# An output product split after nine of its fifteen steps, and rules by slot for a hand-written order: a gated mix of two memory-attention branches on one core

## The chip, the core and the metric

The kernel runs on one core of a Trainium2 chip. Its engines are TensorE (PE in the profile; PEld is its loading of weights), VectorE (DVE), ScalarE (ACT), GpSimd (POOL) and SyncE (SP, which issues every DMA here). The metric is device time of one execution in microseconds.

## What is computed

Two branches, A and B, each do the following with weights of their own. Their results are mixed token by token.

```python
# x: 2048 tokens x 640; 32 heads of 20; 4 segments of 512 tokens
q, k, v = x @ wq, x @ wk, x @ wv
M, z = 0, 0
for s in range(4):
    logits = einsum("hqd,hkd->hqk", qs, ks) * 20 ** -0.5 + causal_mask
    a_dot = softmax(logits) @ vs
    a_mem = (phi(qs) @ M) / (phi(qs) @ z + 1e-6)      # phi(t) = t + 1 if t > 0 else exp(t)
    o = sigmoid(beta) * a_mem + (1 - sigmoid(beta)) * a_dot
    M, z = M + phi(ks).T @ vs, z + phi(ks).sum(tokens)
branch = o @ wo
# after both branches
g = sigmoid((x * gate_w).sum(-1))
out = g * branch_A + (1 - g) * branch_B
```

## The kernel before

**Tiling.** A window t is one branch of one segment: t = 0 to 7, with branch t % 2 and segment t // 2. In a window the 32 heads are taken four at a time; such a group is a quad, i = 0 to 63, eight to a window. The 640 features are five blocks of 128 (k or m = 0 to 4). A product of 640 by 640 with 512 tokens is done block by block: for each output block m it has 15 steps, five blocks k by three terms, because each operand is split into a high and a low part (high x high, low x high, high x low). The products are q, k, v and o of every window.

**Halves.** Most matmuls use only 64 of the 128 rows of the array, so that two streams, one for each half, run at once. `product` (L577) gives a unit whose steps exist once for each half: one half does its steps first, the other follows into the same PSUM bank after a lag, `UP_LAG` (0.3). A step of both halves is costed at `STEP` = 0.2335. `whole` (L160) emits a matmul over all 128 rows.

**One quad.** S units (L962, five to a quad) make scores for the row maximum, which DVE reads (L980). The maxima go through a small transpose and a DMA into two extra rows of `qst` (L1013 to L1033). T units (L1052, five to a quad) make the transposed scores less the maximum; ACT takes the exponential (L1075) and POOL masks it (L1076). They need a place for the result: ten tiles of their own (`own_p`), or rows borrowed from the pool `big` of 27 rows, where `p_room` (L1039) allows that. When all ten masked tiles are there, `pv_unit` (L1091) does the weighted sum with v on the whole array (L1103, 32 matmuls). `fin_unit` (L1146) transposes it back, DVE weights it, and POOL adds it to the memory part in `O`. When the heads of a feature block k are complete, `o_transpose` (L1187) gives the pair `OTs[t, k]`, ready when its low part is subtracted (L1196). The output product of a window reads these five pairs.

**Order.** The program is written by a planner inside the kernel: it runs a clock with costs for each operation, and emits each instruction when its model says that the inputs are there. What is emitted is a fixed order for each engine; nothing is decided on the chip. Products ("jobs", L322 to L327) are filler, taken in order by `fill_gen` (L1224); `marks[i]` says how much filler is done before slot i begins. In slot i the main loop (L1361 on) places the ten units of `ORDER`: T units of quad i, S units of quad i + 2, each after `fill_to` a target, spread over `SPAN` = 1.010 of the slot; the weighted sum of quad i - 1 falls due at its start. Units with low priority (memory reads, updates, transposes for them) are held back while DVE has more than `CALM` = 2.38 us queued (`start_late`, L1244). T units may borrow rows when at least `BORROW` + 2 = 10 are free and nobody waits for rows. These settings are the same in all 66 slots.

**The last output product** (t = 7) has no window behind it to be filler for, so `job_last` (L880) does its five blocks m side by side in five banks, with whole matmuls, k by k as the pairs come:

```python
    yield from hold_on(lambda: (t, KT - 2) in OTs, "last")
    ...
    for k in range(KT):
        yield from hold_on(lambda: (t, k) in OTs, "last")
        ...
        for m in range(KT):
            ...
            for j, (w, o) in enumerate(((wh, oh), (wl, oh), (wh, ol))):
```

The result of branch A for the same segment, already in `part`, is loaded (L890) and added (L901), and the sum is stored (L903).

Of the kernel before, what the change touches and what calls it, by code (L numbers as in the profile page):

```python
# [12 lines left out]
F32 = mybir.dt.float32  # L13
# [29 lines left out]
def tile_gated_mix_infini_attn(  # L43
# [43 lines left out]
    idle = []  # L87
    DONE = {"A": 0.14, "D": 0.11, "G": 0.1, "S": 0.0}
# [69 lines left out]
    UP_LAG = 0.3  # L158
# [147 lines left out]
    BORROW = 8  # L306
# [20 lines left out]
    jobs += [(7, "last", m) for m in range(KT)]  # L327
# [3 lines left out]
    def cost(kind):  # L331
        return 60 * STEPV if kind == "v" else 15 * STEP
# [28 lines left out]
    def stage(i):  # L361
# [3 lines left out]
        t, kind, m = jobs[i]  # L365
        src = weights[t % 2][kind if kind in "qkv" else "o"]
# [29 lines left out]
        def got(w):  # L396
            w3 = w.rearrange("p (k n) -> p k n", n=P)

            def landed():
                if kind == "last" and m == KT - 1:  # L400
                    wvhl.want(1, lambda pair: split_hi(tuple(x[:, :, :P] for x in pair)))
                else:
                    whl.want(1, split_hi, prio=i)
# [475 lines left out]

    def job_last(t):  # L880

        s = t // 2
        yield from hold_on(lambda: (t, KT - 2) in OTs, "last")
        parts, pps = {}, {}
        for m in range(KT):
            def got_pt(tile, m=m):
                if (s, m) not in part_there:
                    at(clk[0] + 0.5, lambda: got_pt(tile, m))
                    return
                dma(0.7, lambda: nc.sync.dma_start(  # L890
                    out=r32(tile), in_=part[s][P * m:P * (m + 1), :]), lambda: parts.__setitem__(m, tile))

            big.want((F32,), got_pt, prio=3)

        def finish(m):
            def got(ot):
                def take():
                    if m not in parts:
                        at(clk[0] + 0.3, take)
                        return  # L900
                    put("D", 0.63, lambda: nc.vector.tensor_tensor(  # L901
                        out=r32(ot), in0=pps[m], in1=r32(parts[m]), op=ALU.add), lambda: dma(
                            0.7, lambda: nc.sync.dma_start(  # L903
                                out=outT[P * m:P * (m + 1), L * s:L * (s + 1)], in_=r32(ot)), prio=2), prio=2)

                take()

            big.want((F32,), got, prio=2)

        for k in range(KT):  # L910
            yield from hold_on(lambda: (t, k) in OTs, "last")
            oh, ol = OTs[t, k]
            for m in range(KT):
                i = job_index[t, "last", m]
                yield from hold_on(lambda: i in split, "split")
                wh, wl = split[i]
# [3 lines left out]
                for j, (w, o) in enumerate(((wh, oh), (wl, oh), (wh, ol))):  # L920
                    yield from hold_on(lambda: not any((*firsts, *seconds, *lane_ops)), "last")
                    whole(STEP, lambda: nc.tensor.matmul(  # L922
                        pps[m], lhsT=w[:, k, :], rhs=o, start=(k == 0 and j == 0), stop=(k == KT - 1 and j == 2)))
# [115 lines left out]
    def p_room():  # L1039
        return len(own_p) > 1 or len(big.free) >= BORROW + 2 and not big.queue  # L1040

# [169 lines left out]
    def begin(i):  # L1211
# [3 lines left out]
        if kind == "last" and m == 0:  # L1215
            for j in range(i, len(jobs)):
                stage(j)
# [6 lines left out]
    def fill_gen():  # L1224
        for i, (t, kind, m) in enumerate(jobs):
# [7 lines left out]
            if i < len(HEAD0):  # L1233
# [4 lines left out]
                        "last": lambda: job_last(t) if m == 0 else ()}[kind]()  # L1238
# [5 lines left out]
    def start_late(keep):  # L1244
        for x in late:
            prio, _, cost, ok, fn = x
            if len(bank.free) <= (0 if prio <= 0 else keep) or (prio > 2 and load["D"] > CALM):
                continue
# [4 lines left out]
    def start_unit(half):  # L1253

        u = start_late(KEEP)
# [11 lines left out]
    def lane_step(half):  # L1267
# [24 lines left out]
        if u:  # L1292
# [3 lines left out]
            if not u["ops"][half]:  # L1296
                firsts[half] = None
                u["at"] = lane[half] + UP_LAG
# [45 lines left out]
    CALM, KEEP, UNIT = 2.38, 0, 1  # L1344
    ORDER = "TSTSTSTSTS"
    SPAN = 1.010
# [14 lines left out]
    for i in range(66):  # L1361
        fill_to(marks[i])
        if i == 0:
            for j in range(LEAD):
                for n in range(5):
                    when_ready(UNIT, S(j, n), "S")
# [3 lines left out]
        todo = list(ORDER if i else "TSTSTSTSTS")  # L1370
        at_ = {"S": 0, "T": 0}
        for j in range(len(ORDER)):
            fill_to(marks[i] + SPAN * (j + 1) / len(ORDER) * (marks[i + 1] - marks[i]))
# [66 lines left out]
```

## Time and profile before

| | |
|---|---|
| median of three runs | 1073.05 us (1070.78 to 1073.85) |
| the profiled execution | 1072.62 us, span 1070.8 us |
| granted TensorE clock, mean | 0.998 |
| busy: PE, PEld, DVE, ACT, POOL | 1054.6, 885.3, 763.2, 658.1, 584.3 us |
| HBM read, written | 131.43 MB, 73.40 MB |

The span is the time from the first to the last instruction of the program, and the profiled execution's own time has what lies around it as well. Busy times are unions of an engine's instructions. Ends of matmuls are modelled, so a busy PE may still be fed thinly.

### The profile page before, as it was taken

To read this page: it belongs to the slowest core of one execution; us is meant where nothing else is said; L and a number is where in the kernel's file an instruction comes from. 1 tells how busy PE (TensorE), PEld (TensorE's weight loads), DVE (VectorE), ACT (ScalarE), POOL (GpSimd) and SP (SyncE) were. 2 spreads that over 40 slices of the span, in tenths; PEclk is the share of its full clock that TensorE was granted. 3 is DMA by queue.
4 is the path that set the end of the run, shared out by engine and by line. 5 is a ranking of instruction groups with operands and counts; after the bars stand their busy time and mean duration, and the time that the engine had idled before them with its cause. 6 is when DMAs were issued, how large, how long until landed. Compare 5 with 4: busy or idle time off the path is not lost.

```text
span 1070.8 us, 31710 instructions
## 1 busy us (share of the span) xinstructions
PE 1054.6 (98%) x11689; PEld 885.3 (83%) x11689; DVE 763.2 (71%) x2724; ACT 658.1 (61%) x1330; POOL 584.3 (55%) x1045
## 2 busy tenths in 40 slices
PE   7999999999999999999999999999999999999998
PEld 6877888988989889888798888888878887889855
DVE  3597776659767698665887768856777867877751
ACT  5276656668665576655765557655665657576670
POOL 4273636467364574566645557555764537555470
PEclk9999999999999999999999999999999999999999
DMA  6985587477565786664847468657575765857521
GB/s 235 308 282 146 192 242 216 129 236 241 157 202 146 197 273 189 195 196 141 253 144 220 150 180 275 179 180 228 146 229 164 238 179 170 253 167 194 166 83 49
DMA packets 110026, 207.95 MB, mean 194 GB/s; under 512 B 12464, under 2 KB 16560, under 8 KB 109872
## 3 DMA queue, kind: packets, MB, share of 16 engines
q1 hardware_dynamic: 109872, 205.93, 63.8%
q8 instruction: 92, 1.51, 0.6%
q14 instruction: 62, 0.51, 0.2%
HBM read 131.43 MB, written 73.40 MB: 191 GB/s over the span
## 4 chain that ended last, share of the span: by engine, by line
PE 93%; DMA 2%; ACT 2%; DVE 1%; POOL 1%; issue 1%; SPq 0%; ACTq 0%; POOLq 0%; DVEq 0%
PE bank L580 52%; PE bank L1103 13%; PE bank L993 7%; PE bank L1083 7%; PE bank L724 4%; PE bank L764 3%; PE bank L686 3%; PE bank L922 2%; PE bank L625 1%; DMA row<-in_xT_dram 1%; ACT p L1075 1%; DVE bank L980 1%; DMA kst<-kd 1%; PE bank L1018 1%; DMA wst<-in_a_wk_dram 0%
## 5 line engine op out<-in xcount | busy, mean ns | idle before, releaser
L980 DVE CUSTOM_DVE_ANT_0 bank<-bank,tri 128x384 f32<-128x384 f32 (+3 forms) x1024 | 475.7, 519 | 160.6 <-PE bank L993 134.1
L580 PE MATMUL bank<-row,wh 64*128 64x512 f32 x2220 | 509.6, 406 | 1.2 <-ACT p L1075 0.5
L1075 ACT ACTIVATE p<-bank 128x512 f32<-128x512 f32 x602 | 330.8, 599 | 171.4 <-PE bank L1083 136.5
L1076 POOL TENSOR_SCALAR_AFFINE_SELECT p<-p 128x256 f32<-128x256 f32 (+1 forms) x602 | 219.1, 372 | 279.1 <-ACT p L1075 268.1
L580 PEld LDWEIGHTS bank<-row,wh 64*128 64x128 f32 x2220 | 312.0, 186 | 17.9 <-issue 3.4
L580 PE MATMUL bank<-row,wl 64*128 64x512 f32 x1110 | 292.9, 400 | 0.0
L409 POOL TENSOR_TENSOR wl<-wst,wh 128x640 fp32r<-128x640 f32 x115 | 180.0, 1570 | 49.8 <-ACT wh L407 49.4
L580 PE MATMUL bank<-wvh,row 64*128 64x320 f32 x1280 | 201.7, 316 | 0.3 <-ACT p L1075 0.3
L993 PE MATMUL bank<-kst,qst 60*128 60x384 f32 (+3 forms) x1024 | 183.2, 321 | 0.1
L1083 PE MATMUL bank<-qst,kst 62*128 62x384 f32 (+3 forms) x1024 | 179.5, 320 | 0.2
L580 PEld LDWEIGHTS bank<-row,wl 64*128 64x128 f32 x1110 | 166.6, 185 | 7.0 <-issue 1.2
L580 PEld LDWEIGHTS bank<-wvh,row 64*128 64x128 f32 x1280 | 161.5, 185 | 3.5 <-issue 1.6
L1103 PE MATMUL bank<-p,vst 128*32 128x128 f32 (+3 forms) x1964 | 151.2, 434 | 0.0
L980 DVE DVE_READ_ACCUMULATOR2_ANT mx<- 128x1 f32 x1024 | 145.1, 142 | 0.0
L993 PEld LDWEIGHTS bank<-kst,qst 60*128 60x128 f32 x1024 | 127.9, 185 | 10.3 <-issue 1.6
L1083 PEld LDWEIGHTS bank<-qst,kst 62*128 62x128 f32 x1024 | 127.9, 185 | 9.0 <-issue 1.6
L1103 PEld LDWEIGHTS bank<-p,vst 128*32 128x32 f32 x1964 | 59.7, 110 | 88.1 <-issue 64.0
L580 PE MATMUL bank<-wvl,row 64*128 64x320 f32 x640 | 113.5, 312 | 0.0
L407 ACT CAST wh<-wst 128x640 fp32r<-128x640 f32 x119 | 85.5, 738 | 23.7 <-PE bank L580 11.9
L580 PEld LDWEIGHTS bank<-wvl,row 64*128 64x128 f32 x640 | 88.2, 185 | 0.8 <-issue 0.6
L549 DVE TENSOR_TENSOR row<-bank,row 128x512 fp32r<-128x512 f32 x80 | 54.8, 688 | 36.8 <-ACT row L537 17.7
L724 PE MATMUL bank<-ident,row 64*128 64x64 f32 x752 | 79.6, 226 | 1.2 <-DVE mx L980 0.8
(91 smaller groups left out, 1252.5 us busy)
## 6 DMA issues: line engine op xcount, KB each, us to landing
qd<-row SPq DMA_DIRECT2D x120, 256.0 KB
kd<-row SPq DMA_DIRECT2D x120, 256.0 KB
qst<-qd SPq DMA_DIRECT2D x128, 240.0 KB
kst<-kd SPq DMA_DIRECT2D x128, 240.0 KB
wst<-in_a_wq_dram SPq DMA_DIRECT2D x20, 320.0 KB
wst<-in_a_wk_dram SPq DMA_DIRECT2D x20, 320.0 KB
wst<-in_b_wq_dram SPq DMA_DIRECT2D x20, 320.0 KB
wst<-in_b_wk_dram SPq DMA_DIRECT2D x20, 320.0 KB
```

The source lines that it names most:

```text
L407: put("A", 0.66, lambda: nc.scalar.copy(wh, w3), lambda: put(lo_eng, lo_cost, lambda: lo.tensor_tensor(out=wl, in0=w3, in1=r32(wh), op=ALU ...
L409: lambda: lo.tensor_tensor(out=wl, in0=w3, in1=r32(wh), op=ALU.subtract), end, prio=3), prio=6)
L549: put("D", 0.63, lambda: nc.vector.tensor_tensor(out=lo, in0=src, in1=r32(hi), op=ALU.subtract), out, prio=1)
L580: return nc.tensor.matmul(bank_of, lhsT=w[ROWS[half]], rhs=x_[ROWS[half]], start=start, stop=stop)
L686: return nc.tensor.matmul(pm[:, a - h0:c - h0, :].rearrange("p h e -> p (h e)"), lhsT=r32(pqTs[t, m][ROWS[half], P * n:P * (n + 1)]), rhs= ...
L724: return nc.tensor.transpose(px[:, n, r], block(n)[r], ident[r, r])
L980: put("D", w / 960.0 + 0.112, lambda: nc.vector.tensor_tensor_reduce(out=sc[:, off:off + w], in0=sc[:, off:off + w], in1=tri[:, L - w:], s ...
L993: lane_ops[half].append((w * 0.000458, lambda pair=pair, qb=qb, off=off, w=w, r=r, sc=sc: nc.tensor.matmul(sc[:, off:off + w], lhsT=q[r, p ...
L1075: put("A", 0.49, lambda: nc.scalar.activation(pt, sc, AF.Exp, scale=SCALE), lambda: (bank.give(sc), put("G", 0.05 + 0.16 * len(todo), lamb ...
L1076: "G", 0.05 + 0.16 * len(todo), lambda: nc.gpsimd.affine_select(out=blocks, in_=blocks, pattern=[[0, len(todo)], [1, P]], base=0, channel_ ...
L1083: lane_ops[half].append((w * 0.000458, lambda pair=pair, kb=kb, off=off, w=w, r=r, sc=sc: nc.tensor.matmul(sc[:, off:off + w], lhsT=k[r, p ...
L1103: nc.tensor.matmul(po[32 * j:32 * j + 32, P * kb:], lhsT=vst[t % 2][:, kb, h * E1:h * E1 + 32], rhs=pts[i, n, f][0][:, off:off + w], start ...
```

## The change

The jobs of the last product become five "early" ones, one for each m, and one "last". An early job is an ordinary product of nine steps: k = 0, 1, 2 (`SOON` = 3), both halves of the array, due as soon as the first three pairs exist. Its sum is added to the row of `part` on DVE, kept in that row (`kept`), and its bank is given back. The job "last" then does the other six steps of each m side by side as before, and adds its banks to the kept rows in place. The special staging of all weights at the start of the last product goes: the weights come by the look-ahead of four jobs, as for others.

The constants `ORDER`, `SPAN`, `CALM`, `UP_LAG` and `BORROW` become fields of a table, `RULES`, by slot, in the order: order of units, span, calm, lag, room. A rule holds until a later slot has one. `KEEP` and `UNIT` are replaced by their values.

```diff
@@ -85,6 +85,46 @@
     load = {e: 0.0 for e in "ADGS"}
     dma_free = [0.0, 0.0]
     idle = []
+
+
+    RULES = {
+        0: "TSTSTSTSTS 1.010 2.38 0.30 4",
+        2: "SSTSTSTSTT 1.010 2.38 0.41 4",
+        3: "TSTSTSTSTS 0.932 2.38 0.30 8",
+        5: "TSTSTSTSTS 0.947 2.38 0.30 8",
+        6: "TSTSTSTSTS 1.010 1.90 0.26 8",
+        7: "TTSSTTSSTS 1.010 1.62 0.40 8",
+        9: "TSTSTSTSTS 1.010 2.38 0.30 8",
+        15: "TSTSTSTSTS 0.994 2.09 0.32 4",
+        16: "TSTSTSTSTS 1.029 2.38 0.37 8",
+        17: "TSTSTSTSTS 1.010 2.38 0.31 8",
+        18: "TSTSTSTSTS 0.936 3.13 0.30 8",
+        23: "TTSTSTSTSS 0.931 2.38 0.41 4",
+        24: "TSTSTSTSTS 1.010 2.38 0.30 8",
+        26: "TSTSTSTSTS 0.941 2.69 0.31 8",
+        28: "TSTSTSTSTS 0.947 3.15 0.30 8",
+        30: "TSTSTSTSTS 1.010 2.38 0.30 8",
+        31: "STSTSTSTST 0.948 3.28 0.30 6",
+        32: "TSTSTSTSTS 0.997 2.38 0.30 8",
+        33: "TSTSTSTSTS 1.010 3.21 0.30 8",
+        35: "TSTSTSTSTS 1.010 2.38 0.30 8",
+        39: "SSTSTSTSTT 1.010 2.38 0.30 4",
+        41: "TSTSTSTSTS 1.010 2.38 0.30 8",
+        44: "TSTSTSTSTS 0.971 2.38 0.30 8",
+        48: "TSTSTSTSTS 1.010 2.38 0.30 8",
+        49: "TSSTTSSTTS 1.010 2.38 0.38 8",
+        50: "TSTSTSTSTS 1.010 2.38 0.30 8",
+        51: "TSTSTSTSTS 1.010 2.38 0.38 8",
+        54: "TSTSTSTSTS 1.010 2.38 0.30 8",
+        56: "TSSTTSSTTS 1.010 2.38 0.30 8",
+        59: "TSTSTSTSTS 1.010 3.16 0.33 8",
+        60: "SSSTSTSTTT 0.922 1.82 0.30 8",
+        61: "TTSSTTSSTS 1.010 3.55 0.27 8",
+        62: "TSTSTSTSTS 1.010 2.38 0.30 8",
+        63: "SSTSTSTSTT 1.010 2.38 0.30 8",
+        65: "SSTSTSTSTT 0.950 2.38 0.36 8",
+    }
+    rule = {}
     DONE = {"A": 0.14, "D": 0.11, "G": 0.1, "S": 0.0}
 
     def at(time, fn):
@@ -155,7 +195,6 @@
     lane_ops = [deque(), deque()]
     firsts = [None, None]
     seconds = [deque(), deque()]
-    UP_LAG = 0.3
 
     def whole(dur, emit):
         now[0] = max(now[0], lane[0], lane[1]) + dur
@@ -303,7 +342,6 @@
     wvhl = Store([tuple(sb.tile([P, KT, VN], F32R, tag=f"wv{c}", name=f"wv{c}", bufs=1) for c in "hl")])
 
     own_p, pts = list(range(10)), {}
-    BORROW = 8
 
 
     HEAD0 = [("q", 0), ("k", 0), ("q", 1), ("k", 1)]
@@ -324,12 +362,14 @@
     jobs = [(0, kind, m) for kind, m in HEAD0]
     for t in range(8):
         jobs += window_jobs(t)
-    jobs += [(7, "last", m) for m in range(KT)]
+    jobs += [(7, "early", m) for m in range(KT)]
+    jobs += [(7, "last", 0)]
+    SOON = 3
     job_index = {j: i for i, j in enumerate(jobs)}
 
 
     def cost(kind):
-        return 60 * STEPV if kind == "v" else 15 * STEP
+        return 60 * STEPV if kind == "v" else 3 * SOON * STEP if kind == "early" else 15 * STEP
 
     def window_cost(t):
         return sum(cost(kind) for _, kind, _ in window_jobs(t))
@@ -363,6 +403,8 @@
             return
         staged.add(i)
         t, kind, m = jobs[i]
+        if kind == "last":
+            return
         src = weights[t % 2][kind if kind in "qkv" else "o"]
         lo_eng, lo = ("D", nc.vector) if i < 4 else ("G", nc.gpsimd)
         lo_cost = 0.9 if i < 4 else 1.6
@@ -397,7 +439,7 @@
             w3 = w.rearrange("p (k n) -> p k n", n=P)
 
             def landed():
-                if kind == "last" and m == KT - 1:
+                if kind == "early" and m == KT - 1:
                     wvhl.want(1, lambda pair: split_hi(tuple(x[:, :, :P] for x in pair)))
                 else:
                     whl.want(1, split_hi, prio=i)
@@ -877,50 +919,65 @@
 
         yield from product(pp, terms, STEP, done)
 
+    kept = {}
+
+    def job_early(t, m):
+
+        i = job_index[t, "early", m]
+        s = t // 2
+        pt = []
+
+        def got_pt(tile):
+            if (s, m) not in part_there:
+                at(clk[0] + 0.5, lambda: got_pt(tile))
+                return
+            dma(0.7, lambda: nc.sync.dma_start(
+                out=r32(tile), in_=part[s][P * m:P * (m + 1), :]), lambda: pt.append(tile), prio=need[i] + 4)
+
+        big.want((F32,), got_pt, prio=3)
+        yield from hold_on(lambda: i in split and all((t, k) in OTs for k in range(SOON)), "OT")
+        yield from hold_on(lambda: len(bank.free) > 0, "bank")
+        pp = bank.free.pop(0)
+        wh, wl = split[i]
+        terms = [
+            (lambda w=w, c=c, k=k: (w[:, k, :], OTs[t, k][c])) for k in range(SOON) for w, c in ((wh, 0), (wl, 0), (wh, 1))
+        ]
+
+        def take():
+            if not pt:
+                at(clk[0] + 0.3, take)
+                return
+            put("D", 0.63, lambda: nc.vector.tensor_tensor(
+                out=r32(pt[0]), in0=pp, in1=r32(pt[0]), op=ALU.add), lambda: (bank.give(pp), kept.__setitem__(m, pt[0])), prio=2)
+
+        yield from product(pp, terms, STEP, take)
+
     def job_last(t):
 
         s = t // 2
-        yield from hold_on(lambda: (t, KT - 2) in OTs, "last")
-        parts, pps = {}, {}
-        for m in range(KT):
-            def got_pt(tile, m=m):
-                if (s, m) not in part_there:
-                    at(clk[0] + 0.5, lambda: got_pt(tile, m))
-                    return
-                dma(0.7, lambda: nc.sync.dma_start(
-                    out=r32(tile), in_=part[s][P * m:P * (m + 1), :]), lambda: parts.__setitem__(m, tile))
-
-            big.want((F32,), got_pt, prio=3)
+        pps = {}
 
         def finish(m):
-            def got(ot):
-                def take():
-                    if m not in parts:
-                        at(clk[0] + 0.3, take)
-                        return
-                    put("D", 0.63, lambda: nc.vector.tensor_tensor(
-                        out=r32(ot), in0=pps[m], in1=r32(parts[m]), op=ALU.add), lambda: dma(
-                            0.7, lambda: nc.sync.dma_start(
-                                out=outT[P * m:P * (m + 1), L * s:L * (s + 1)], in_=r32(ot)), prio=2), prio=2)
-
-                take()
-
-            big.want((F32,), got, prio=2)
-
-        for k in range(KT):
+            if m not in kept:
+                at(clk[0] + 0.3, lambda: finish(m))
+                return
+            put("D", 0.63, lambda: nc.vector.tensor_tensor(
+                out=r32(kept[m]), in0=pps[m], in1=r32(kept[m]), op=ALU.add), lambda: dma(
+                    0.7, lambda: nc.sync.dma_start(
+                        out=outT[P * m:P * (m + 1), L * s:L * (s + 1)], in_=r32(kept[m])), prio=2), prio=2)
+
+        for k in range(SOON, KT):
             yield from hold_on(lambda: (t, k) in OTs, "last")
             oh, ol = OTs[t, k]
             for m in range(KT):
-                i = job_index[t, "last", m]
-                yield from hold_on(lambda: i in split, "split")
-                wh, wl = split[i]
+                wh, wl = split[job_index[t, "early", m]]
                 if m not in pps:
                     yield from hold_on(lambda: bank.free, "bank")
                     pps[m] = bank.free.pop(0)
                 for j, (w, o) in enumerate(((wh, oh), (wl, oh), (wh, ol))):
                     yield from hold_on(lambda: not any((*firsts, *seconds, *lane_ops)), "last")
                     whole(STEP, lambda: nc.tensor.matmul(
-                        pps[m], lhsT=w[:, k, :], rhs=o, start=(k == 0 and j == 0), stop=(k == KT - 1 and j == 2)))
+                        pps[m], lhsT=w[:, k, :], rhs=o, start=(k == SOON and j == 0), stop=(k == KT - 1 and j == 2)))
                     yield STEP
                 if k == KT - 1:
                     after_whole(lambda m=m: finish(m))
@@ -1037,7 +1094,7 @@
         return split_unit(*ops, lambda: mr_store.want(1, got))
 
     def p_room():
-        return len(own_p) > 1 or len(big.free) >= BORROW + 2 and not big.queue
+        return len(own_p) > 1 or len(big.free) >= rule["room"] + 2 and not big.queue
 
     def p_place(i, n, half):
         if own_p:
@@ -1212,9 +1269,6 @@
         t, kind, m = jobs[i]
         for j in range(i, i + AHEAD + 1):
             stage(j)
-        if kind == "last" and m == 0:
-            for j in range(i, len(jobs)):
-                stage(j)
         if kind == "q" and m == 2:
             ask_gates(t)
         if kind == "v" and m == 4 and t % 2 and t < 7:
@@ -1235,7 +1289,7 @@
                 continue
             yield from {"q": lambda: job_qk(t, kind, m), "k": lambda: job_qk(t, kind, m),
                         "v": lambda: job_v(t, m // 4), "o": lambda: job_o(t, m),
-                        "last": lambda: job_last(t) if m == 0 else ()}[kind]()
+                        "early": lambda: job_early(t, m), "last": lambda: job_last(t)}[kind]()
 
     fill = fill_gen()
     filled = [0.0]
@@ -1244,7 +1298,7 @@
     def start_late(keep):
         for x in late:
             prio, _, cost, ok, fn = x
-            if len(bank.free) <= (0 if prio <= 0 else keep) or (prio > 2 and load["D"] > CALM):
+            if len(bank.free) <= (0 if prio <= 0 else keep) or (prio > 2 and load["D"] > rule["calm"]):
                 continue
             if ok():
                 late.remove(x)
@@ -1252,7 +1306,7 @@
 
     def start_unit(half):
 
-        u = start_late(KEEP)
+        u = start_late(0)
         if u is None and not over[0]:
             u = next(fill, -1.0)
             if u == -1.0:
@@ -1295,7 +1349,7 @@
             filled[0] += u["credit"]
             if not u["ops"][half]:
                 firsts[half] = None
-                u["at"] = lane[half] + UP_LAG
+                u["at"] = lane[half] + rule["lag"]
                 (seconds[1 - half].append if u["credit"] else seconds[1 - half].appendleft)(u)
         return True
 
@@ -1341,9 +1395,11 @@
         t, u = divmod(i, 8)
         return p_done.get(i) == 10 and (t, "v", u // 4) in arrived
 
-    CALM, KEEP, UNIT = 2.38, 0, 1
-    ORDER = "TSTSTSTSTS"
-    SPAN = 1.010
+    def rules(i):
+        if i in RULES:
+            order, rule["span"], rule["calm"], rule["lag"], rule["room"] = RULES[i].split()
+            rule.update({x: float(rule[x]) for x in rule if x != "order"}, order=order)
+
 
     put("G", 6.0, small_tiles, prio=0)
     put("G", 1.6, ones_tiles, prio=1)
@@ -1359,18 +1415,19 @@
         dma(0.9, lambda b=b: nc.sync.dma_start(out=bts[b], in_=betas[b].partition_broadcast(P)), betas_there, prio=marks[0] - 8)
     dma(0.84, lambda: nc.sync.dma_start(out=gw, in_=gate_w.partition_broadcast(P)), prio=marks[0] - 6)
     for i in range(66):
+        rules(i)
         fill_to(marks[i])
         if i == 0:
             for j in range(LEAD):
                 for n in range(5):
-                    when_ready(UNIT, S(j, n), "S")
+                    when_ready(1, S(j, n), "S")
                     s_unit(j, n)
         if 1 <= i < 65:
             pv_due.append(i - 1)
-        todo = list(ORDER if i else "TSTSTSTSTS")
+        todo = list(rule["order"])
         at_ = {"S": 0, "T": 0}
-        for j in range(len(ORDER)):
-            fill_to(marks[i] + SPAN * (j + 1) / len(ORDER) * (marks[i + 1] - marks[i]))
+        for j in range(10):
+            fill_to(marks[i] + rule["span"] * (j + 1) / 10 * (marks[i + 1] - marks[i]))
             c = todo[0]
             if c == "S" and i + LEAD < 64 and "T" in todo and not S(i + LEAD, 0)() and T(i, 0)():
                 c = "T"
@@ -1378,7 +1435,7 @@
             n = at_[c]
             at_[c] += 1
             if i + (LEAD if c == "S" else 0) < 64:
-                when_ready(UNIT, S(i + LEAD, n) if c == "S" else T(i, n), c)
+                when_ready(1, S(i + LEAD, n) if c == "S" else T(i, n), c)
                 if c == "S":
                     s_unit(i + LEAD, n)
                 else:
```

## Rows read from the trace of the kernel before

**Rows 1.** The page: span, TensorE's busy time, and the engines' shares of the chain.
```profile
span 1070.8 us, 31710 instructions
...
PE 1054.6 (98%) x11689; PEld 885.3 (83%) x11689; DVE 763.2 (71%) x2724; ACT 658.1 (61%) x1330; POOL 584.3 (55%) x1045
...
PE 93%; DMA 2%; ACT 2%; DVE 1%; POOL 1%; issue 1%; SPq 0%; ACTq 0%; POOLq 0%; DVEq 0%
```

**Rows 2.** The chain of work in the body, 60 to 1028 us, by line.
```profile
by line: PE bank L580 54.3%; PE bank L1103 14.3%; PE bank L993 7.7%; PE bank L1083 7.5%; PE bank L724 4.1%; PE bank L764 3.1%; PE bank L686 3.0%; DMA row<-in_xT_dram 1.2%; ACT p L1075 0.7%; DVE bank L980 0.7%; DMA kst<-kd 0.6%; issue 0.5%; 
```

**Rows 3.** The chain in order of time: start, length, piece.
```profile
737.47 5.91 DMA row<-in_xT_dram
...
915.30 5.61 DMA kst<-kd
...
1017.62 2.29 PE bank L1103 x32
```

**Rows 4.** The body in fourteen stretches: length, busy times, PEclk, DMA share, GB/s.
```profile
69.00:138.00 69.00, 67.73 (x796) 55.08 (x791) 54.47 (x199) 46.41 (x97) 40.19 (x79) 1.00 0.65 198
...
552.00:621.00 69.00, 69.00 (x813) 59.92 (x811) 47.93 (x174) 38.88 (x79) 37.24 (x72) 1.00 0.61 182
...
sum 959.00, PE 955.63 PEld 809.42 DVE 710.94 ACT 611.40 POOL 543.61; mean PE 68.26 PEld 57.82 DVE 50.78 ACT 43.67 POOL 38.83
```

**Rows 5.** Timeline of the end: start, length, engine, line, operation, idle before it.
```profile
1027.94 0.39 PE L580 MATMUL bank<-row,wh 64*128 64x512 f32 x1
...
1033.18 0.69 DVE L1196 TENSOR_TENSOR row<-bank,row 128x512 fp32r<-128x512 f32 x1 [1.79 <-ACT row L1196]
...
1034.48 0.14 PEld L1103 LDWEIGHTS bank<-row,vst 128*32 128x32 f32 x2 [1.01 <-POOL row L1076]
1034.67 2.24 SPq L890 DMA_DIRECT2D row<-part  x5
...
1037.07 1.29 PE L1083 MATMUL bank<-qst,kst 62*128 62x512 f32 x12
...
1037.69 5.01 ACT L1075 ACTIVATE p<-bank 128x512 f32<-128x512 f32 x10
...
1041.51 1.85 POOL L1076 TENSOR_SCALAR_AFFINE_SELECT p<-p 128x256 f32<-128x256 f32 x5
...
1042.94 3.73 PE L1103 MATMUL bank<-p,vst 128*32 128x512 f32 x32
...
1051.40 0.97 PE L724 MATMUL bank<-ident,O 64*128 64x64 f32 x8
...
1053.02 0.69 DVE L1196 TENSOR_TENSOR row<-bank,row 128x512 fp32r<-128x512 f32 x1 [2.96 <-ACT row L1196]
1063.60 3.44 DVE L901 TENSOR_TENSOR row<-bank,row 128x512 f32<-128x512 f32 x5 [9.88 <-PE bank L922]
```

**Rows 6.** The end in stretches; columns as in rows 4.
```profile
1037.00:1043.00 6.00, 4.10 (x45) 2.83 (x41) 0.92 (x3) 5.80 (x12) 3.92 (x12) 1.00 0.49 165
1043.00:1047.00 4.00, 4.00 (x34) 1.71 (x34) 0.69 (x1) 0.49 (x2) 0.35 (x1) 0.60 0.02 4
...
1052.30:1066.35 14.05, 14.01 (x62) 11.19 (x60) 3.44 (x6) 0.59 (x1) 0.00 (x0) 1.00 0.08 31
1066.35:1071.00 4.65, 0.00 (x0) 0.00 (x0) 0.69 (x1) 0.00 (x0) 0.00 (x0) 1.00 0.56 187
```

**Rows 7.** The last pieces of the chain, from 1046 us on.
```profile
1046.67 1.39 PE bank L922 x4
...
1048.97 2.50 PE bank L922 x10
...
1052.37 13.96 PE bank L922 x60
```

## The prediction

> **What bounds the kernel now.** I read the page first. TensorE is busy for 98% of the span and the chain that ended last runs through it for 93% [rows 1], so what can change the time is how densely TensorE is fed, and how the chain ends. The second view is the chain over the body, 60 to 1028 us: its seven TensorE groups add up to 94%, and no other piece has more than 1.2% [rows 2]. Single late pieces do exist there: a load of x of 5.91 us before 743 us, a load of kst of 5.61 us [rows 3]. TensorE kept working during them, so they are not 11.5 us of idle time. As a busy TensorE isn't one at its peak, I took the busy time of the weight loads as a measure of how many matmuls a stretch got through. The body cut into fourteen stretches holds 809.42 us of loads in 959 us; the thinnest stretch has 55.08 in 69 us, the densest 59.92 [rows 4].
>
> The third view is the end. The last matmul of an ordinary output product starts at 1027.94; the tile OT(7,2) is complete with the subtraction at 1033.18, so at 1033.87. Then TensorE stands in the weighted sum of quad 62, behind masks, and gets to the T units of quad 63 at 1037.07. Their ten exponentials last until 1042.70, their masks until 1043.36. The weighted sum of quad 63 starts at 1042.94 and takes 3.73 us, and OT(7,4) is complete at 1053.71 [rows 5]. An earlier weighted sum took 2.29 us [rows 3]: between 1037 and 1043 TensorE was busy for 4.10 of 6 us, after which the granted clock averaged 0.60 over 1043 to 1047 [rows 6], that is, it ran at the lower of its levels (1.2 GHz) for most of that time. Of the 75 side-by-side steps of the last product only 15 were done by 1052.37; the other 60 took 13.96 us in one piece, 0.2327 us each [rows 7]. TensorE ends at 1066.35, and 4.65 us of additions and stores follow [rows 6]. So the end is bound by 75 steps that start late, not by the tiles they wait for.
>
> **Part 1, the split of the last product.** Before, nothing of it may run until OT(7,3) exists. Now the terms of k = 0, 1, 2 (45 of the 75 steps) are five ordinary products that need OT(7,0) to OT(7,2) alone, thus from 1033.87; 30 steps stay side by side. Nothing is removed from TensorE: 45 whole matmuls become 90 half ones, two of which run at once, 2 x 9 a product. Added are five additions on DVE (0.69 us each, from the five at the end in 3.44 us [rows 5]); DVE is busy for 0.92 us between 1037 and 1043 [rows 6], which covers them. Without that cover one could put off the subtraction that completes a tile by 0.69 us. The five loads of part stay five, on SP's queue, where they were issued from 1034.67 on [rows 5]; nothing is moved past another queue's work. Each early product holds its bank until its rows have landed.
>
> What it gains: from 1037.07 to 1052.3 there are 15.2 us. In them stand the T units (1.29 us for 12 of the 16 matmuls [rows 5], so 1.7), the weighted sum (2.3 at the full clock) and four groups of eight transposes (0.97 each alone [rows 5]; about 0.6 beside a product on the other half, my estimate, so 2.4; 3.9 at most). That leaves 8.8 us (7.3), or 38 steps (31) at 0.2327 us, where 15 were done. So 37 to 44 steps remain, 8.6 to 10.2 us, and TensorE ends at 1060.9 to 1062.5 in place of 1066.35: a gain of 3.9 to 5.4 us. I take 5. The far bounds: OT(7,4) is there at 1053.71, some 1.4 us earlier with the full clock, and 15 steps of k = 4 must follow (3.5 us), hence 1055.8 at best, a gain of 10.5; and 0 if nothing gets into the hole. Between 1060.9 and 1055.8 there are 5.1 us by which quad 63 may come later at no cost.
>
> Moving work from the whole form to the half form is priced at nothing: the 60 whole steps hold 11.19 us of weight loads inside 14.05 us in which TensorE is busy for 14.01 [rows 6], so their loads lie beside the matmuls already. The Trainium skill says otherwise (TensorE: Matmul & The Clock Gate, Part 3: Packing small matmuls): a weight load overlaps running matmuls only where it goes to another group of rows. By that rule whole steps would pay for their loads and half steps would not, and the sum would come out lower by what 45 loads cost. The measured 0.2327 us a step disagrees with it here.
>
> **Part 2, the table of rules.** It adds and removes no instruction: each slot still has five T and five S units and the same products. It changes their order, the share of a slot over which they are spread (0.922 to 1.029), the DVE load above which low-priority units wait (1.62 to 3.55), the lag of a second half (0.26 to 0.41), and the number of free rows above which T units may borrow (4, 6 or 8). A rule stays until the next, so 45 of the 66 slots differ from the old constants. As the order written out depends on what came before, the body is arranged anew from the first slots on. The rows don't show that arrangement, so I bound it. All stretches as dense as the best: 809.42 x 69 / 59.92 = 932.1, 26.9 us less than 959. All as thin as the worst: 1014.0, 55 us more. A mere re-draw: thinnest and densest lie 4.84 apart in a mean of 57.8, or 5.8 us of time in 69; fourteen values with such a range scatter by about 1.7 us, so their sum by 1.7 x 3.74 = 6.4 us. The settings reach two thirds of the slots, so of the 26.9 us some 18; I take a third of that, 6 us, about one scatter to the good side, because the change of order can reach only what waits for place and order, not the fixed cost of joining both halves for the 64 weighted sums. The ends kept for the range are 16 us of gain and 12 of loss.
>
> **The sum.** The profiled execution took 1072.62 us, a span of 1070.8 and 1.8 around it; the median of the runs is 1073.05, 0.4 above, so one number serves both. 1072.6 - 5 - 6 = 1061.6.
>
> **Rivals.** (A) The forecast, both parts gain: 1052 to 1069, chance 0.55. (B) The table re-draws without gain and only the end gains: 1067.6, chance 0.20. For it: the body is 94% TensorE on the chain. Against: the thin stretches. (C) The hole isn't filled and the table gives nothing: 1072.6, chance 0.07. Early products hold banks until the part rows land, the DMA engines are busy for 0.49 of the time from 1037 to 1043 [rows 6], and T units of quad 63 need two banks each. It decides when they come more than 5.1 us later. (D) The re-draw falls one scatter to the bad side: 1074, chance 0.06. (E) Slower: with the borrowing bound at 4 in slot 23 and in slots 39 and 40, T units take rows that the loads of x for the next segment are about to ask for, and the first q products wait for x. Its price is a load as late as the 5.91 us piece [rows 3] at both places: 1067.6 + 11.8 = 1079.4; it decides from 8.7 us of such waits on. For it: the load of x is already on the chain. Against: TensorE had other work then, and T units can't borrow once a load is queued. Chance 0.10. (F) Weight loads of whole steps count in full: 45 x 0.187 us = 8.4 less, 1053. The 60 steps in 13.96 us speak against it: 0.187 us of open load would leave 0.046 for 512 columns. Chance 0.02. That is the result by the Trainium skill's rule above.
>
> **How the numbers follow.** About 0.3%, 3.2 us, is what a measurement of this kernel can tell from no change: faster is below 1069.9, slower above 1076.3. Faster: A, F and three quarters of B, 0.72. Same: the rest of B, C and half of D, 0.15. Slower: E and half of D, 0.13. The likeliest is A's 1061.6, with 1052 to 1069 of its own; 1050 to 1073 takes in B and C and leaves out E, most of D and the far end of A.
>
> **What would show it.** Right: half matmuls on the OT rows between 1034 and 1052, no stretch at the lower clock there, a weighted sum of quad 63 near 2.3 us, at most some 40 steps in the last unbroken piece, and 4.65 us behind them as before; in the body, the same busy times of every group and more weight loads a stretch. Wrong: T units of quad 63 waiting for banks or rows; DVE's additions ahead of the subtractions; the first weighted sums of the last window starting later than before, which is the table's loss; x or kst loads as longer pieces of the chain. The forecast fails most easily in the table's 6 us, the one term without a row of its own.

## The result, and the profile after

The changed kernel took 1055.43 us (median of four runs, 1054.98 to 1055.97) beside 1072.11 for the kernel before: a ratio of 0.9844, interval 0.9826 to 0.9861, or 16.7 us of 1072. The forecast was 1061.6, faster, with 1050 to 1073 as its range. Ratios below are all to the kernel before, and a gain in us is worked out from the ratio with 1072 us.

The page of the changed kernel, the lines that answer to [rows 1]:

```profile
span 1053.3 us, 31761 instructions
...
PE 1041.6 (99%) x11734; PEld 882.2 (84%) x11734; DVE 760.5 (72%) x2723; ACT 663.1 (63%) x1336; POOL 584.9 (56%) x1045
...
PE 94%; DMA 2%; issue 1%; POOL 1%; DVE 1%; SPq 1%; ACT 0%; POOLq 0%; ACTq 0%
```

TensorE has 45 more matmuls, the halves of the early products, and 13 us less of busy time. The other engines' busy times hardly moved; the table adds no work.

The body of the changed kernel in the same stretches as [rows 4]:

```profile
69.00:138.00 69.00, 68.91 (x829) 56.76 (x829) 52.99 (x202) 49.11 (x103) 41.60 (x81) 1.00 0.68 207
...
552.00:621.00 69.00, 69.00 (x811) 60.41 (x810) 49.13 (x177) 39.01 (x78) 37.44 (x74) 1.00 0.59 179
...
sum 959.00, PE 957.91 PEld 814.21 DVE 709.71 ACT 624.21 POOL 553.06; mean PE 68.42 PEld 58.16 DVE 50.69 ACT 44.59 POOL 39.50
```

The numbers in parentheses are counts. The sum of the weight loads (PEld) rose by only 4.8 us, but its last stretch doesn't compare: the changed body ends at 1018, as the timeline below shows, and what follows has fewer loads. Up to 966 us both kernels are in their bodies; here is that stretch in one piece, first before, then changed:

```profile
69.00:966.00 897.00, 893.69 (x10257) 756.81 (x10252) 664.96 (x2382) 570.79 (x1156) 510.42 (x910) 1.00 0.66 197
```

```profile
69.00:966.00 897.00, 896.03 (x10392) 765.25 (x10390) 666.89 (x2403) 583.09 (x1177) 518.09 (x918) 1.00 0.66 200
```

That is 135 more matmuls (1.3%) and 8.4 us more of weight loads (1.1%) in the same 897 us.

The chain of the changed kernel in its body by line, beside [rows 2]:

```profile
by line: PE bank L622 56.2%; PE bank L1160 14.9%; PE bank L1050 8.1%; PE bank L1140 8.0%; PE bank L766 4.2%; PE bank L728 3.4%; PE bank L806 3.3%; DMA wst<-in_x_dram 0.7%; PE bank L1075 0.5%; SPq L1008 0.2%; DVE bank L1037 0.1%; issue 0.1%;
```

The loads of x rows for the products (row<-in_xT_dram, 1.2% before), of kst, and ACT's exponentials are gone from this list; the one load that is left is that of x for the token gates.

The timeline of the end of the changed kernel (start, length, instruction), beside [rows 5]:

```profile
1018.06 0.39 PE L622 MATMUL bank<-row,wh 64*128 64x512 f32 x1
...
1018.46 0.69 DVE L1253 TENSOR_TENSOR row<-bank,row 128x512 fp32r<-128x512 f32 x1 [1.69 <-ACT row L1253]
...
1034.78 2.36 PE L1160 MATMUL bank<-p,vst 128*32 128x512 f32 x32
...
1039.45 1.29 DVE L950 TENSOR_TENSOR row<-bank,row 128x512 f32<-128x512 f32 x2 [0.45 <-PE bank L622]
...
1043.12 0.97 PE L766 MATMUL bank<-ident,O 64*128 64x64 f32 x8
...
1044.75 0.69 DVE L1253 TENSOR_TENSOR row<-bank,row 128x512 fp32r<-128x512 f32 x1 [3.04 <-ACT row L1253]
```

Its stretches, beside [rows 6] (length, busy PE, PEld, DVE, ACT, POOL, then the granted clock):

```profile
1030.00:1034.80 4.80, 4.80 (x56) 4.37 (x52) 1.90 (x6) 3.80 (x8) 3.78 (x10) 1.00 0.00 0
1034.80:1037.20 2.40, 2.40 (x36) 1.05 (x37) 0.55 (x1) 0.00 (x0) 0.00 (x0) 1.00 0.00 0
...
1041.70:1048.80 7.10, 7.00 (x33) 4.68 (x31) 3.46 (x7) 0.59 (x1) 0.88 (x1) 1.00 0.17 62
1048.80:1054.00 5.20, 0.00 (x0) 0.00 (x0) 0.69 (x1) 0.00 (x0) 0.00 (x0) 0.73 0.50 167
```

And the last side-by-side pieces of its chain, beside [rows 7]:

```profile
1040.23 2.96 PE bank L979 x12
...
1044.09 1.92 PE bank L979 x6
```

The reader is to see two gains. The last ordinary step starts at 1018.06 in place of 1027.94 [rows 5]: the body is 9.9 us shorter. From there to the end of the span it is 35.2 us in place of 42.9: the end is 7.6 us shorter. The hole before the weighted sum of quad 63 is full (4.80 of 4.80 us), that sum takes 2.36 us in place of 3.73, at the full clock, and of the 60 steps that stood in one piece at the end 30 are left side by side, 12 before the last transposes and 18 behind them. The end is now set by the last tile, ready at 1045.44, and by the 15 steps that need it.

### The profile page after: what moved, and what is told of

It reads as the page before. It is cut to its first block, busy times and chain, and to the rows that moved or that the text cites. A ratio compares the mean times of both kernels' runs of the same rounds, so it can differ in the third digit from the quotient of the medians.

```text
span 1053.3 us, 31761 instructions
## 1 busy us (share of the span) xinstructions
PE 1041.6 (99%) x11734; PEld 882.2 (84%) x11734; DVE 760.5 (72%) x2723; ACT 663.1 (63%) x1336; POOL 584.9 (56%) x1045
## 4 chain that ended last, share of the span: by engine, by line
PE 94%; DMA 2%; issue 1%; POOL 1%; DVE 1%; SPq 1%; ACT 0%; POOLq 0%; ACTq 0%
PE bank L622 54%; PE bank L1160 14%; PE bank L1050 8%; PE bank L1140 7%; PE bank L766 4%; PE bank L806 3%; PE bank L728 3%; DMA kst<-kd 1%; DMA wst<-in_a_wk_dram 1%; DMA wst<-in_x_dram 1%; POOL wl L451 1%; PE bank L1075 0%; DMA wst<-in_a_wq_dram 0%; PE bank L979 0%; DVE row L964 0%
## 5 line engine op out<-in xcount | busy, mean ns | idle before, releaser
L622 PE MATMUL bank<-row,wh 64*128 64x512 f32 x2268 | 547.8, 405 | 0.1
L622 PEld LDWEIGHTS bank<-row,wh 64*128 64x128 f32 x2268 | 331.7, 185 | 16.1 <-issue 3.3
L622 PE MATMUL bank<-row,wl 64*128 64x512 f32 x1134 | 316.2, 400 | 0.0
L622 PEld LDWEIGHTS bank<-row,wl 64*128 64x128 f32 x1134 | 179.4, 185 | 7.4 <-issue 2.2
L1050 PE MATMUL bank<-kst,qst 60*128 60x128 f32 (+3 forms) x1024 | 181.0, 320 | 0.5 <-DVE mx L1037 0.3
L1140 PE MATMUL bank<-qst,kst 62*128 62x128 f32 (+3 forms) x1024 | 178.8, 319 | 0.0
L622 PEld LDWEIGHTS bank<-wvh,row 64*128 64x128 f32 x1280 | 159.1, 185 | 3.7 <-issue 2.4
L1160 PE MATMUL bank<-p,vst 128*32 128x128 f32 (+3 forms) x1956 | 147.2, 430 | 0.0
L1050 PEld LDWEIGHTS bank<-kst,qst 60*128 60x128 f32 x1024 | 128.5, 185 | 10.2 <-DVE mx L1037 1.7
L622 PE MATMUL bank<-wvl,row 64*128 64x320 f32 x640 | 109.6, 310 | 0.0
L1185 ACT COPY row<-bank 128x512 f32<-128x512 f32 x57 | 33.6, 589 | 80.2 <-PE bank L1160 73.1
```

Source lines behind the costliest of these rows:

```text
L622: return nc.tensor.matmul(bank_of, lhsT=w[ROWS[half]], rhs=x_[ROWS[half]], start=start, stop=stop)
L1050: lane_ops[half].append((w * 0.000458, lambda pair=pair, qb=qb, off=off, w=w, r=r, sc=sc: nc.tensor.matmul(sc[:, off:off + w], lhsT=q[r, p ...
L1140: lane_ops[half].append((w * 0.000458, lambda pair=pair, kb=kb, off=off, w=w, r=r, sc=sc: nc.tensor.matmul(sc[:, off:off + w], lhsT=k[r, p ...
L1160: nc.tensor.matmul(po[32 * j:32 * j + 32, P * kb:], lhsT=vst[t % 2][:, kb, h * E1:h * E1 + 32], rhs=pts[i, n, f][0][:, off:off + w], start ...
L1185: either(0.52, lambda: nc.scalar.copy(r32(oT), po), 0.63, lambda: nc.vector.tensor_copy(r32(oT), po), end, 2)
```

## The experiments

Theory 1: the two parts of the change each do their own work, the split in the end, the table in the body. Rival, theory 2: the split only pays because the table's last rules bring the last quads forward. On the table itself, theory 1a: its settings are good one by one. Theory 1b: it fits one arrangement as a whole, and any other is a new draw.

### One part alone

The first keeps the split and gives the table one rule (its edit is against the changed kernel, like those further down); the second puts the table into the kernel before.

```diff
 e1_split_alone
     RULES = {
-        0: "TSTSTSTSTS 1.010 2.38 0.30 4",
-        ...
+        0: "TSTSTSTSTS 1.010 2.38 0.30 8",
     }
 e2_table_alone, against the kernel before: the table, its fields in place of the constants, as in
-        todo = list(ORDER if i else "TSTSTSTSTS")
+        todo = list(rule["order"])
     (the last product is left as it was)
```

> The split of the last product with the old constants in all 66 slots. If the two parts add up (theory 1), it gains the predicted 5 us of the end and leaves the body alone: about 1067 us (1062 to 1068), last ordinary step at 1028 as before, weighted sum of quad 63 near 2.3 us. If the split needs the table (rival, theory 2: the table brings the last quads forward, without it the pairs come too late), it gains 2 us at most: 1070 or more, and a gap without work before quad 63 stays.

> The table of rules with the old last product, all 15 steps side by side. Theory 1: the body is shorter by about 10 us, as the last ordinary step ended at 1018.4 in place of 1028.3 after the change, and the end as long as before: about 1062 us (1060 to 1064). Theory 2: the parts need each other, the table alone gains less than 8 us: 1064 or more, as its work is done earlier only to wait at the end.

The split alone took 1065.31 us, ratio 0.9929 (0.9913 to 0.9944), a gain of 7.6 us. The table alone took 1062.80, ratio 0.9907 (0.9892 to 0.9922), a gain of 10.0. The product of the two ratios is 0.9837; both together measured 0.9844. They add up, as theory 1 has it. In the split alone the last ordinary step and the subtraction that completes OT(7,2) stand here:

```profile
1026.51 0.39 PE L588 MATMUL bank<-row,wh 64*128 64x512 f32 x1
...
1032.45 0.68 DVE L1219 TENSOR_TENSOR row<-bank,row 128x512 fp32r<-128x512 f32 x1
```

These pieces of its chain are early steps, the weighted sum of quad 62, that of quad 63, and the side-by-side steps behind the last transposes:

```profile
1031.87 2.34 PE bank L588 x17
1034.21 2.29 PE bank L1126 x32
...
1044.06 2.29 PE bank L1126 x32
...
1051.98 4.11 PE bank L945 x17
```

The weighted sum of quad 63 is at the full clock, though it starts 1 us later than before (1042.94 [rows 5]). Of the 30 side-by-side steps one ran before the last transposes; the chain follows the other 29 as far as the 17th, where the additions take over. From the last ordinary step to the end of the span at 1063.3 it is 36.8 us in place of 42.9, a gain of 6.1. The other 1.4 us between these two traces were there before the split could act: the first stores of q go out at 21.24 us (second line) in place of 22.84. That differs from execution to execution; in the changed kernel's trace it is 22.92, and over the traces of all runs 20.64 to 23.72.

```profile
22.84 1.29 SPq L562 DMA_DIRECT2D qd<-row  x3
```

```profile
21.24 1.31 SPq L570 DMA_DIRECT2D qd<-row  x3
```

With the table alone the products' last step and the last piece of the chain read as follows, the first from the view of one line's instructions (durations, then first and last start):

```profile
L616 PE MATMUL bank<-row,wh x2220: 383/393/512, 29.6 to 1017.7; 64*128 64x512 f32 x185
```

```profile
1044.10 12.13 PE bank L958 x52
```

The body ends 10.2 us earlier than before, and from 1017.7 to the span's end at 1060.8 it is 43.1 us, as long as the 42.9 before. So the table's whole gain lies in the body. Without the split the hole and the low clock stay; the stretches of the table alone (the clock is the last but two):

```profile
1028.00:1034.00 6.00, 3.81 (x16) 2.65 (x17) 1.57 (x4) 3.73 (x8) 2.99 (x8) 0.59 0.10 37
1034.00:1037.00 3.00, 3.00 (x15) 1.85 (x17) 0.00 (x0) 0.20 (x1) 0.59 (x2) 0.69 0.00 0
```

### The table by slots

```diff
 e3_rules_to_58
+        59: "TSTSTSTSTS 1.010 2.38 0.30 8",
-        59: "TSTSTSTSTS 1.010 3.16 0.33 8",
-        ...
 e4_rules_from_59
+        0: "TSTSTSTSTS 1.010 2.38 0.30 8",
-        0: "TSTSTSTSTS 1.010 2.38 0.30 4",
-        ...
         59: "TSTSTSTSTS 1.010 3.16 0.33 8",
```

> Split and table, but the rules of slots 59 to 65 replaced by the old constants. If the table's gain lies in the body (theory 1): 1056 to 1058. If it lies in the order of the last quads, which comes to the end (theory 2): 1062 or more.

> Split, and the table in slots 59 to 65 alone. Theory 1: as the split alone, 1067 within 2 us. Theory 2: most of the gain, 1060 or less.

Rules up to slot 58: 1056.37 us, 0.9843 (0.9826 to 0.9860), the same as all. Rules from slot 59 on: 1068.36 us, 0.9963 (0.9952 to 0.9974), 3.6 us worse than no rules beside the split. Theory 2 falls: the last seven slots' rules give nothing that can be measured behind the arrangement they stand in, and cost something behind another.

### The table by settings, and moved

```diff
 e5_order_only, e6_span_only, e7_room_only: one column of the table (slot 2 of the first shown)
-        2: "SSTSTSTSTT 1.010 2.38 0.41 4",
+        2: "SSTSTSTSTT 1.010 2.38 0.30 8",
 e8_shift_8: the rules of slots 0 to 58 eight slots later, the last eight slots' at the front
-        2: "SSTSTSTSTT 1.010 2.38 0.41 4",
+        10: "SSTSTSTSTT 1.010 2.38 0.41 4",
```

> Split, and of the table the orders of units alone, the other four columns at the old constants. Theory 1a, the table's 9 us come from settings that are good one by one: each column keeps a share, this one some 3 us, so 1062. Theory 1b, the table fits as a whole one arrangement of the body, and a part of it is a re-draw: anywhere within 6.4 us of the split alone, 1059 to 1072, with no share to be told.

> Split, and of the table the spans alone (0.922 to 1.029). Theory 1a: the units of a slot come earlier wherever the span is below 1.010, some 4 us of the 9 stay, so 1061. Theory 1b: 1059 to 1072, a draw.

> Split, and of the table the free rows that T units leave alone (4, 6 or 8). Theory 1a: some 2 us of the 9, so 1063. Theory 1b: 1059 to 1072. The rival of the prediction with late loads of x: 1070 or more, with loads of x on the chain.

> Split, and the whole table moved on by eight slots, one window (the rules of slots 59 to 65 in place): each rule acts on the same quad of the next window. Theory 1a, the settings are good wherever they stand: at least half of the 9 us stays, 1060 or less. Theory 1b, fitted: the gain over the split alone is lost, 1065 within one scatter of 6.4 us, as likely above as below.

| the split and | us | ratio, interval | against the split alone | matmuls, 69 to 966 us |
|---|---|---|---|---|
| the orders | 1089.62 | 1.0171 (1.0148 to 1.0193) | +26 us | 10111 |
| the spans | 1074.67 | 1.0023 (1.0011 to 1.0034) | +10 us | 10195 |
| the rooms | 1071.50 | 0.9997 (0.9986 to 1.0008) | +7 us | 10225 |
| the table, eight slots later | 1099.20 | 1.0255 (1.0232 to 1.0278) | +35 us | 9998 |

The fourth column is the difference of the ratio to 0.9929, times 1072. The last is TensorE's count in the view shown above for before and after (10257 and 10392); the split alone has 10265. The slower the run, the fewer matmuls it has in the same stretch; at 0.087 us for each, about half of the loss or more is there by 966 us. Theory 1a falls: none of the three columns tried keeps a share of the gain, each of them alone loses, and the table moved by a window loses most. The held-back load (`CALM`) and the lag weren't tried alone. Theory 1b was right in kind and far too narrow: it had allowed 1059 to 1072, and three of the four lie above that, by 3, 18 and 27 us. The rooms alone came to 1071.5 with no load of x rows among the longest pieces of their chain, so the late loads of x weren't what made them slower.

### One number moved by a hundredth

```diff
 e12_nudge
-        2: "SSTSTSTSTT 1.010 2.38 0.41 4",
+        2: "SSTSTSTSTT 1.010 2.38 0.40 4",
```

> After, with one number changed: the lag of slot 2 from 0.41 to 0.40. The order written out differs from there on. Theory 1a (settings good one by one): nothing to be measured, 1055 within 2. Theory 1b (the table fits one arrangement, and whatever moves an early instruction re-draws the rest): most of the table's 9 us is lost, 1062 or more.

It took 1087.35 us, 1.0132 (1.0108 to 1.0155): 31 us more than the changed kernel, for a hundredth of a microsecond in the planner's lag in one slot of 66. The order written out for TensorE begins the same and differs from early on. This decides for theory 1b: a setting that is worth something by itself doesn't lose 31 us by a hundredth.

Where this arrangement loses can be seen in part. Over the body up to 966 us, and over one stretch of it, the nudged kernel reads:

```profile
69.00:966.00 897.00, 894.78 (x10091) 758.68 (x10090) 644.50 (x2328) 568.31 (x1147) 500.99 (x892) 0.99 0.64 194
...
621.00:690.00 69.00, 68.52 (x720) 55.80 (x717) 44.07 (x146) 39.36 (x80) 36.62 (x58) 1.00 0.75 227
```

It has 301 matmuls fewer than the changed kernel's 10392, or 2.9%, some 26 us' worth; its weight loads are only 0.9% less. From 621 to 690 us the changed kernel has 787 matmuls where these are 720, at the full clock in both, so a good part of the loss has nothing to do with the clock. In another place it has: first the nudged kernel, then the changed one, in the same 20 us, 178 matmuls in place of 246:

```profile
310.00:320.00 10.00, 9.64 (x98) 7.65 (x95) 5.00 (x17) 4.74 (x10) 4.17 (x7) 0.90 0.63 192
320.00:330.00 10.00, 9.93 (x80) 9.43 (x81) 5.10 (x13) 3.10 (x7) 0.59 (x2) 0.59 0.41 128
```

```profile
310.00:320.00 10.00, 10.00 (x123) 8.17 (x121) 7.54 (x24) 5.03 (x12) 3.46 (x8) 1.00 0.69 193
320.00:330.00 10.00, 10.00 (x123) 9.00 (x123) 8.67 (x34) 5.48 (x11) 4.76 (x8) 1.00 0.37 102
```

Between 320 and 330 the nudged kernel's TensorE reads 9.93 us busy and 9.43 us of weight loads, more than the changed kernel's 9.00, and did 80 matmuls in place of 123: at a clock of 0.59 each of them lasts longer and fills the row. Two microseconds at a time (nudged kernel), what went before:

```profile
316.00:318.00 2.00, 1.72 (x13) 1.57 (x14) 0.00 (x0) 1.14 (x3) 0.58 (x2) 1.00 0.95 241
318.00:320.00 2.00, 2.00 (x13) 2.00 (x13) 1.02 (x4) 0.00 (x0) 0.00 (x0) 0.51 0.99 258
...
326.00:328.00 2.00, 2.00 (x18) 2.00 (x17) 0.26 (x2) 0.37 (x1) 0.00 (x0) 0.50 0.36 133
```

At 316.22 a train of twenty memory-read matmuls begins with no product on the other half; 13 matmuls are in two microseconds, and from 318 the clock is at its lower level, 1.2 GHz, to 328. Ten microseconds at half the clock cost 5 us at most here, a sixth of the 31.

### The form and the size of the early products

```diff
 e9_early_whole
-        yield from product(pp, terms, STEP, take)
+        for n, term in enumerate(terms):
+            yield from hold_on(lambda: not any((*firsts, *seconds, *lane_ops)), "early")
+            w, x_ = term()
+            whole(STEP, lambda: nc.tensor.matmul(pp, lhsT=w, rhs=x_, start=(n == 0), stop=(n == len(terms) - 1)))
+            yield STEP
+        after_whole(take)
 e10_soon_2, e11_soon_4
-    SOON = 3
+    SOON = 2
     (SOON = 4 in the second)
```

> After, with the early products as whole matmuls over 128 rows in place of two halves; the same 45 steps at the same place. Theory 1, a step costs the same in both forms: 1055 to 1060, the excess being what both halves wait for each other at the joins. Rival (weight loads of whole steps aren't overlapped): 45 x 0.187 = 8.4 us more in the steps themselves, 1064 or more, and whole steps in the hole further apart than 0.2327 us.

> After, with two blocks k in the early products (30 steps) and nine steps side by side (45). Theory 1, the hole before quad 63 is filled by what has no wait: fewer early steps, and the 45 late ones can fill only where both halves are free: 1056 to 1060. Rival (the size of the early part doesn't matter, the gain is the table's): 1055 within 1.

> After, with four blocks k in the early products (60 steps): they need OT(7,3), which came at 1039.0 in the changed kernel, so nothing of the last product can run before. Theory 1: the hole is back, 75 steps x 0.2327 = 17.5 us follow from 1039 and 4.5 us of stores, 1061 of span, 1063. Rival: 1055 within 1.

Early products as whole matmuls: 1057.89 us, 0.9863 (0.9842 to 0.9883), some 2 us over the changed kernel, with intervals that overlap. Two pieces of their chain:

```profile
1022.10 2.95 PE bank L956 x12
...
1039.74 2.49 PE bank L956 x10
```

That is 0.25 us a step, against the 0.2327 of [rows 7], so the price of nothing for the form was right within 0.02 us a step. A weight load of 0.187 us (11.19 us for 60 [rows 6]) that had to be waited for would leave 0.06 us of such a step for its 512 columns, and the rival's 8.4 us aren't there. The Trainium skill (TensorE: Matmul & The Clock Gate, Part 3: Packing small matmuls) states that a load overlaps running matmuls only where it goes to another group of rows. These 128-row steps don't agree with it.

With two blocks early: 1057.61 us, 0.9863 (0.9844 to 0.9881), some 2 us over. That is in theory 1's range, but the intervals overlap, so two and three blocks aren't told apart with certainty. With four: 1063.91 us, 0.9918 (0.9898 to 0.9937), 7.9 us over, the gain of the split gone. The hole is back, with its low clock (0.65, third from the end):

```profile
1028.00:1037.00 9.00, 6.60 (x47) 4.72 (x49) 1.61 (x4) 5.39 (x11) 4.31 (x11) 0.65 0.13 46
```

The number came out as expected by a somewhat different way: OT(7,3) was there some 5 us earlier than the 1039 that I had put in, but the early steps that followed it ran at the lower clock at first.

## Why the prediction was right, and where it was off

**What bounds the kernel** was read rightly: TensorE's feed in the body, and 75 steps that start late at the end. Both moved.

**The split, 5 us.** The mechanism is shown step by step: hole filled, weighted sum at 2.36 us, no low clock there, the last unbroken piece down from 60 steps to 18, about 4.5 us (1048.76 to 1053.3) of additions and stores left as before. The term was mis-sized: 7.6 us (6.0 to 9.3) in place of 3.9 to 5.4. In the two traces 1.4 us of it were there from the first stores of q on, so 6.1 are the end's. The step that failed is the start of the count at 1037.07, as if nothing early could run before TensorE was through the weighted sum of quad 62. In the split alone OT(7,2) was complete at 1033.13, hardly earlier than the 1033.87 before, but early steps began at 1031.87, and 17 half matmuls, 8.5 steps or 2.0 us, ran ahead of that sum. From its end at 1036.50 to 1051.98 another 37.5 steps were done, inside the 31 to 38 counted, so 29 were left in place of 37 to 44. In the changed kernel, with the table, OT(7,2) was complete at 1019.15, 0.7 us after the last ordinary step, where it had been 5.5 us before. The four-block run shows how much hangs on this hole. Half form against whole form made no difference that could be measured, and DVE's additions stood ahead of no completing subtraction: the last of them ended at 1040.74, the subtraction started at 1044.75.

**The table, 6 us.** Its sign came out and its size was 10.0 us (8.4 to 11.6). The step behind it doesn't stand. It took a mere re-draw to scatter by 6.4 us around the kernel before, and placed this table one scatter to the good side. Measured, six other draws lay 4 to 35 us above the split alone, and none below it: four parts of the table, the moved one and the nudged one. (The rules up to slot 58 aren't counted: they keep the body's arrangement.) These draws weren't centred on the constants of before, and they scattered several times as far. The far bounds, 26.9 us of gain and 55 of loss, held; the scatter was too small, and it rested on a measure that hardly tells arrangements apart. Busy time of weight loads is a union, which differs by 0.9% between the nudged and the changed kernel where their matmuls differ by 2.9%, and even rises when the clock falls (9.43 against 9.00). So the table's sign didn't follow from the rows of before, and that it came out was luck as far as the prediction goes; an order for which nothing in the trace spoke gave the larger half of the gain. The rival of a worse re-draw, with a chance of 0.06 and a loss of 6.4 us, was too rare and too small: of the arrangements tried most were slower than the split alone by more than that.

**The other rivals.** That only the end gains (1067.6) is the split alone, at 1065.3. Late loads of x: the changed kernel's chain in the body has none of the loads of x rows left (before 1.2% [rows 2]), so the price was never paid. A hole that stays: not seen with three blocks, seen with four.

**What stays open.** Which rules remove which waits in the body can't be told from parts of the table, since each part is another arrangement. Most of the nudged kernel's loss isn't put down to single waits either. How the table was found, and whether others as good are near it, wasn't tried.

## What to carry to other kernels

Where an order is written out by a planner with feedback, every early change draws the rest anew: freeze what stands before the place under study, judge an edit against several arrangements rather than one, and don't read the gain of a tuned table as a property of its settings. Work that hangs on the last inputs only in part should be cut there, so that the rest fills the last wait: the cut belongs at the input that arrives while there is still something to wait for (three blocks here, two at much the same time; with four the gain was gone). Count matmuls per stretch and look at the granted clock before trusting a busy time.

## What the runs showed of the hardware that I had not expected

The granted clock can fall in the middle of a body in which TensorE reads 96% busy: in the nudged kernel (9.64 of 10 us from 310 to 320) it went to 0.51 at 318 us after a stretch of 2 us with 13 matmuls, and TensorE ran at 1.2 GHz to 328. Whole 128-row steps of 512 columns that follow one another keep their weight loads hidden: 0.2327 us a step in the kernel before, 0.25 in the run with whole early products.
